# A piece of wq in a transfer of its own, and another order of the last steps, in a decode step of windowed attention with a gated MLP

## The chip, the cores and the metric

The kernel runs on one core of one Trainium2 chip. It is one launch: all inputs are in the chip's memory, the output of 4 KB goes back there. The metric is device time in microseconds (us), taken as the median of several runs. The profile is one execution recorded by the hardware profiler: which instruction ran when on TensorE (PE, with its weight loads PEld), VectorE (DVE), ScalarE (ACT), GpSimd (POOL) and SyncE (SP), what each waited for, and every packet that the 16 DMA engines moved.

## The reference

Two tokens (batch B = 2, one position each) of D = 512 pass through a layernorm, then two branches, all in float32:

```python
xn = _layernorm(x)                                   # 2 x 512
# A: attention of 32 query heads over 8 kv heads, last W = 4096 of 32768 positions
q = (xn @ wq)                                        # 512 x 4096, heads of 128
k = k_cache[:, :, Sk - W:, :]; v = v_cache[:, :, Sk - W:, :]
o = softmax(q @ k^T * 128 ** -0.5) @ v               # 4 query heads per kv head
s = o.reshape(B, 1, 4096) @ wo                       # 4096 x 512
# B: a gated MLP of 512 -> 1792 -> 896 -> 512
z = gelu(xn @ w_in); z1, z2 = halves(z); z2 = layernorm(z2) * w_sp + b_sp
g = silu((z1 * z2) @ w_out)
out = x + s * g
```

What must be read: 2 x 8 windows of K and of V at 2 MB each (64 MB), wq and wo at 8 MB each, w_in 3.5 MB, w_out 1.75 MB: some 89 MB. The arithmetic is small beside that.

## The kernel before

**Tiles and buffers.** The big loads go through a ring of four buffers of 32 KB a partition (`slot`): `win` (w_in), `wq0` and `wq2` (two of wq's four row sets each), the tiles `k` and `v` of eight units, `wo0` and `wo1`. `w_out` has a buffer of another pool. A unit is two of the sixteen (batch, kv head) pairs; its K and its V are 4 MB each, one transfer each (`load`, L134).

**wq.** Row 4p + k of wq lies on partition p (`wq_v`, L125), so each of the four sets k is 128 rows of 4096 columns. The layernormed x is transposed by four small PE transposes into `xnT` (L195 to L198), whose set k holds the same 128 rows; `queries(k)` (L262) multiplies set k with eight blocks of 512 columns and adds up over k in PSUM. wq0 (k = 0, 1) comes in one transfer of 4 MB, wq2 (k = 2, 3) in two of 2 MB:

```python
for k, n in ((0, 2),) if a == 0 else ((0, 1), (1, 1)):
    sp.dma_start(t[:, k : k + n], wq_v[:, a + k : a + k + n, :])
```

From PSUM the queries go through `qs`, `qx`, `xm` and a matmul `qa` into `qb` (`place_queries`, L327), the arrangement in which the score matmuls use them.

**A unit's steps.** `T` (`turn`, L373) transposes an eighth of K on DVE into `kts`; `shares` (L383) multiplies with `qb` on PE into `sh`; `keep` copies to `ss` on ACT; `scores` adds up on PE; `row_max`, `spread_max`, `share_max` and `bias` give the maximum; `exp` (`probs`) is ACT's, `probs_t` DVE's transpose into `pT`; `pv` (L451) multiplies with V into `acc` on PE; `own_sum`, `share_sum`, `weights` give 1/sum; `evacuate` scales on ACT, and `collect` and `gather` put the heads into `o1`.

**wo.** The 32 heads are split into three sets by kv head (`SETS`, L360): set 0 has kv heads 0 to 3 of both tokens, 16 rows of wo on each partition; sets 1 and 2 have two kv heads and 8 rows each. `spread` and `place` turn a set's `o1` into `oT`. `load_wo` (L511) gives out the transfers: set 0 in two halves of 2 MB (tile `wo0`), then in tile `wo1` set 1 in two halves of 1 MB and set 2 in blocks of 4, 2, 1 and 1 rows. `wo_early` (L523) multiplies sets 0 (steps `X`) and 1 (steps `Y`) with full rows of 512 columns into `part`, two rows a step; behind ORDER, the tail (L575 to L594) copies `part` to `parts`, multiplies set 2 into `so` and adds `parts` to it by a matmul with `rowm` after the first block. Then two DVE operations (gate, x) and the store.

**What sets the order.** The string `ORDER` (L27 to L52) lists all steps from unit 0 on; each engine runs its instructions in exactly that order (`InOrder`). `K:u`, `V:u` and `wo:n` stand in it too, and the SP engine gives out all big loads in this order: win, wout, wq, k0, k1, v0, k2, v1 and so on, v7, wo0, wo1. A load waits on SP until its ring buffer has been read for the last time: k2 takes the buffer of wq2 and waits for `queries(3)`, v7 waits for the last `T` of unit 6, wo0 for the last `pv` of unit 5, wo1 for the last `T` of unit 7. What stands behind a waiting load on SP waits too.

Of the kernel before, what the change touches and what calls it, by code (L numbers as in the profile page):

```python
# [9 lines left out]
F32 = mybir.dt.float32  # L10
AF = mybir.ActivationFunctionType
# [3 lines left out]
P = 128  # L15
HQ, DH = 32, 128
G = 4
# [3 lines left out]
def free_ap(t, offset, dims):  # L21

    return bass.AP(tensor=t.tensor, offset=t.offset + offset, ap=[list(t.ap[0])] + [list(d) for d in dims])
# [18 lines left out]
K:6 V:5 T:5.0 T:5.1 T:5.2 rowmax:4.1 mg:4 shmax:4 T:5.3 bias:4 shares:5.0 T:5.4 gather:3 exp:4.0 probs_t:4.0 T:5.5  # L42
T:5.6 exp:4.1 keep:5.0 pv:4.0 lsum:4 shsum:4 scores:5.0 T:5.7 shares:5.1 probs_t:4.1 pv:4.1 weights:4 keep:5.1
scores:5.1 evac:4 col:4 rowmax:5.0
K:7 V:6 T:6.0 rowmax:5.1 T:6.1 mg:5 T:6.2 shmax:5 T:6.3 T:6.4 bias:5 exp:5.0 exp:5.1 T:6.5 shares:6.0 probs_t:5.0
pv:5.0 lsum:5 T:6.6 keep:6.0 probs_t:5.1 T:6.7 shsum:5 scores:6.0 weights:5 shares:6.1 rowmax:6.0 pv:5.1
V:7 T:7.0 wo:0 keep:6.1 evac:5 scores:6.1 col:5 T:7.1 T:7.2 rowmax:6.1 mg:6 shmax:6 gather:5 spread:0 T:7.3 bias:6
T:7.4 T:7.5 shares:7.0 exp:6.0 probs_t:6.0 T:7.6 keep:7.0 pv:6.0 T:7.7 wo:1 exp:6.1 scores:7.0 shares:7.1 probs_t:6.1
keep:7.1 lsum:6 shsum:6 scores:7.1 rowmax:7.0 weights:6 pv:6.1 evac:6 rowmax:7.1 mg:7 shmax:7 col:6 oT:0 bias:7
gather:6 spread:1 exp:7.1 exp:7.0 probs_t:7.1 lsum:7 X:0.1 probs_t:7.0 X:0.3 X:0.2 shsum:7 weights:7 X:0.0 pv:7.0  # L50
pv:7.1 oT:1 evac:7 X:0.7 Y:0.1 X:0.4 X:0.5 col:7 Y:0.0 X:0.6 gather:7 spread:2 oT:2 Y:0.3 Y:0.2
"""  # L52


# [16 lines left out]
def kernel(  # L71
# [14 lines left out]
    pe, dve, act, sp = (InOrder(tc, e) for e in (nc.tensor, nc.vector, nc.scalar, nc.sync))  # L86
    B, _, D = x.shape
# [7 lines left out]
    KT = D // P  # L95
# [3 lines left out]
    DC = D // G  # L99
    SCALE = DH ** -0.5  # L100
    OFF = 30000.0 / SCALE

    fit = ctx.enter_context(tc.tile_pool(name="fit", bufs=1))
    fit.tile([P, 480], F32, tag="fit", name="fit")
# [2 lines left out]
    cst = ctx.enter_context(tc.tile_pool(name="cst", bufs=1))  # L107
    sb = ctx.enter_context(tc.tile_pool(name="sb", bufs=2))
    ps = ctx.enter_context(tc.tile_pool(name="ps", bufs=1, space=bass.MemoryType.PSUM))

    def slot(name, *shape):
        return ring.tile([P, *shape], F32, tag="slot", name=name)

    def bank(name, *shape):
        return ps.tile([P, *shape], F32, tag="kt", name=name, bufs=2)
# [9 lines left out]
    wq_v = wq.rearrange("(p k) f -> p k f", p=P)  # L125
    wqt = []
    for a in range(0, KT, 2):
        t = slot(f"wq{a}", 2, HQ * DH)
        for k, n in ((0, 2),) if a == 0 else ((0, 1), (1, 1)):
            sp.dma_start(t[:, k : k + n], wq_v[:, a + k : a + k + n, :])  # L130
        wqt += [t[:, 0], t[:, 1]]

    wb1 = cst.tile([1, 2], F32, tag="wb1", name="wb1")
# [12 lines left out]
    def load(u, src, name):  # L146
        t = slot(f"{name}{u}", UJ, DH)
        b, v = divmod(u, HKV // 2)
        first = src[b, 2 * v, SK - W, :]
        of = bass.AP(tensor=src.tensor, offset=first.offset, ap=[[UJ * DH, P // 2], [SK * DH, 2], [1, UJ * DH]])  # L150
        sp.dma_start(t.rearrange("p j d -> p (j d)"), of)
        return t


    ident = cst.tile([P, P], F32, tag="ident", name="ident")
    make_identity(nc, ident)
    selw = cst.tile([P, 60], F32, tag="selw", name="selw")
    nc.gpsimd.memset(selw, 0.0)
    xnT = cst.tile([P, KT, 32], F32, tag="xnT", name="xnT")
    nc.gpsimd.memset(xnT, 0.0)  # L160
    ones = cst.tile([P, P], F32, tag="ones", name="ones")
    nc.gpsimd.memset(ones, 1.0)
# [7 lines left out]
    rowm = cst.tile([P, 32], F32, tag="rowm", name="rowm")  # L170
# [21 lines left out]
    rsqrt(rs, va, "x")  # L192
    xn = sb.tile([B, D], F32, tag="o", name="xn", bufs=1)
    dve.tensor_scalar(xn, xs, mv[:, 0:1], rs, op0=ALU.subtract, op1=ALU.mult)
    pt = bank("xnT_ps", KT, B)  # L195
    for k in range(KT):
        pe.transpose(pt[:, k, :], xn.rearrange("b (p k) -> b k p", k=KT)[:, k, :], ident[:B, :B])
    dve.tensor_copy(xnT[:, :, :B], pt)  # L198

    same = cst.tile([P, G, 32], F32, tag="same", name="same")  # L200
# [15 lines left out]
    dve.tensor_reduce(other, free_ap(rowm, 0, [[4, 2], [8, REP]]), axis=AX.X, op=ALU.add)  # L216
    dve.tensor_scalar(other, other, -OFF, OFF, op0=ALU.mult, op1=ALU.add)
    diag = cst.tile([P, 4], F32, tag="diag", name="diag")
# [18 lines left out]
    for n in range(G):  # L237
        pz = bank(f"z{n}", 512)[:, :FC]
        for k in range(KT):
            pe.matmul(  # L240
                pz[32 * k : 32 * k + 32, :], xnT[:, k, :], win[:, k, n * FC : (n + 1) * FC],
                start=True, stop=True,
# [9 lines left out]
    pt = bank("zT_ps", 2, FT, B)  # L252
# [7 lines left out]
    pq = [ps.tile([P, 512], F32, tag=f"s{r}", name=f"q_ps{r}") for r in range(NR)]  # L260

    def queries(k):  # L262
        for r in range(NR):
            for g in range(G):
                c = (r * G + g) * 512
                pe.matmul(
                    pq[r][32 * g : 32 * g + 32, :], xnT[:, k, :], wqt[k][:, c : c + 512],
                    start=(k == 0), stop=(k == KT - 1),
                )

# [3 lines left out]
    u = cst.tile([P, 2, FT, B], F32, tag="u", name="u")  # L274
# [37 lines left out]
    for j in range(FT):  # L312
        for g in range(G):
            pe.matmul(
                y[32 * g : 32 * g + 32, :], hT[:, j, :], wout[:, j, g * DC : (g + 1) * DC],
                start=(j == 0), stop=(j == FT - 1),
# [20 lines left out]
    def place_queries():  # L337
        dve.tensor_tensor(
            free_ap(qb, 16, [[REP, G], [32, NP * G], [1, REP]]), free_ap(qa, 0, [[0, G], [REP, NP * G], [1, REP]]),
            free_ap(grpm, 0, [[1, G], [0, NP * G], [0, REP]]), op=ALU.mult,  # L340
        )

    gate = cst.tile([P, DC], F32, tag="gate", name="gate")

    def silu():
        dve.tensor_scalar(gate, ys, -1.0, 80.0, op0=ALU.mult, op1=ALU.min)
        act.activation(gate, gate, AF.Exp)
        dve.tensor_scalar_add(gate, gate, 1.0)
        dve.reciprocal(gate, gate)
        dve.tensor_mul(gate, gate, ys)  # L350
# [11 lines left out]
    for i, (kv, n, nj) in enumerate(SETS):  # L362
        o1 = cst.tile([P, B, 32], F32, tag=f"o1_{i}", name=f"o1_{i}")
        oT = cst.tile([P, nj, 32], F32, tag=f"oT_{i}", name=f"oT_{i}")
# [102 lines left out]
    col = {}  # L467
# [41 lines left out]
    blocks = []  # L509

    def load_wo(n):  # L511
        t = slot(f"wo{n}", 16, D)
        a = 0
        for i in ((0,), (1, 2))[n]:
            for j, n in (((0, 8), (8, 8)), ((0, 4), (4, 4)), ((0, 4), (4, 2), (6, 1), (7, 1)))[i]:
                sp.dma_start(t[:, a : a + n, :], wo_s[i][:, j : j + n, :])
                blocks.append((t[:, a : a + n, :], sets[f"oT{i}"][1], j))
                a += n
# [4 lines left out]
    def wo_early(n, at):  # L523
        nonlocal done
        if done == 0:
            part.append(ps.tile([P, 512], F32, tag="s0", name="part"))
        t, oT, j = blocks[n]
        for a in range(at, at + 2):
            g = done % G
            pe.matmul(  # L530
                part[0][32 * g : 32 * g + 32, :], oT[:, j + a, :], t[:, a, :], start=(done < G), stop=(done >= EARLY - G)
            )
            done += 1

    part = []
    STEPS = dict(
        T=turn, rowmax=row_max, mg=spread_max, shmax=share_max, bias=bias, exp=probs, probs_t=probs_t, lsum=own_sum,
        shsum=share_sum, weights=weights, shares=shares, keep=keep, scores=scores, pv=pv, evac=evacuate, col=collect,
        gather=gather,
    )  # L540

    def step(name, u, a=()):
        if name == "q":
            place_queries()
        elif name == "silu":
            silu()
        elif name == "K":
            units[u].k = load(u, k_cache, "k")
        elif name == "V":
            units[u].v = load(u, v_cache, "v")  # L550
        elif name == "wo":
            load_wo(u)
        elif name == "spread":
            spread(u)
        elif name == "oT":
            place(u)
        elif name == "X":
            wo_early(a[0] // 4, 2 * (a[0] % 4))
        elif name == "Y":
            wo_early(2 + a[0] // 2, 2 * (a[0] % 2))  # L560
        else:
            STEPS[name](units[u], *a)

    units = []
    for u in range(NU):
        p = Unit()
        p.u, p.m, p.kt, p.sh, p.ss, p.s, p.p, p.pT = u, None, {}, {}, {}, {}, {}, {}
        units.append(p)
    for line in ORDER.strip().split("\n"):
        for name in line.split():  # L570
            name, at = name.split(":")
            u, _, a = at.partition(".")
            step(name, int(u), (int(a),) if a else ())

    parts = sb.tile([P, D], F32, tag="o", name="parts", bufs=1)  # L575
    act.activation(parts, part[0], AF.Copy)
    so = bank("so", DC)
    for n in range(4, len(blocks)):
        t, oT, j = blocks[n]
        for a in range(t.shape[1]):  # L580
            for g in range(G):
                pe.matmul(
                    so[32 * g : 32 * g + 32, :], oT[:, j + a, :], t[:, a, g * DC : (g + 1) * DC],
                    start=(j + a == 0), stop=(j + a == oT.shape[1] - 1),
                )
        if n == 4:
            for g in range(G):
                pe.matmul(
                    so[32 * g : 32 * g + 32, :], rowm, parts[:, g * DC : (g + 1) * DC], start=False, stop=False
                )  # L590
    res = cst.tile([P, DC], F32, tag="res", name="res")
    dve.tensor_mul(res, so, gate)
    dve.tensor_add(res, res, x4)
    sp.dma_start(bass.AP(tensor=out.tensor, offset=out.offset, ap=by_group), res[0 : P : P // (G * B), :])  # L594

# [27 lines left out]
```

## Time and profile before

| | us |
|---|---|
| median of 3 runs (lowest, highest) | 217.93 (217.32, 218.16) |
| the profiled execution's own time | 217.48 |
| its span, first to last instruction | 215.7 |
| PE busy | 143.5 (67%) |
| DVE busy | 126.3 (59%) |
| ACT busy | 50.9 (24%) |
| queue q1 (loads), share of 16 DMA engines' span | 96.6% |
| moved | 89.56 MB, mean 415 GB/s |
| PE's last matmul ends | 212.2 |

The page cuts the span into 40 equal slices and gives a digit of the busy share for each engine, the clock that PE was granted and the mean share of the 16 DMA engines; the windows do the same for any stretch. The chain of waits goes back from the last instruction through what released each. In the timeline, instructions of a group are on one line with start and length; where SP is listed (SPq), the line tells when transfers were given out, not when they moved. A packet is the piece of a transfer that one DMA engine moves as a unit: here one partition's bytes.

### The profile page before, as it was taken

To read this page: it belongs to the slowest core of one execution; us is meant where nothing else is said; L and a number is where in the kernel's file an instruction comes from. 1 tells how busy PE (TensorE), PEld (TensorE's weight loads), DVE (VectorE), ACT (ScalarE), POOL (GpSimd) and SP (SyncE) were. 2 spreads that over 40 slices of the span, in tenths; PEclk is the share of its full clock that TensorE was granted. 3 is DMA by queue.
4 is the path that set the end of the run, shared out by engine and by line. 5 is a ranking of instruction groups with operands and counts; after the bars stand their busy time and mean duration, and the time that the engine had idled before them with its cause. 6 is when DMAs were issued, how large, how long until landed. Compare 5 with 4: busy or idle time off the path is not lost.

```text
span 215.7 us, 2477 instructions
## 1 busy us (share of the span) xinstructions
PE 143.5 (67%) x972; PEld 51.6 (24%) x972; DVE 126.3 (59%) x217; ACT 50.9 (24%) x128; POOL 5.2 (2%) x19
## 2 busy tenths in 40 slices
PE   0179694722864895954990796389168939975993
PEld 0128521300111232312220221122112322221342
DVE  2511212259598989849918972993698199534001
ACT  4111203200114236023330603142032305242020
POOL 8000000000000000000000000000000000000000
PEclk9998578785589699995796589579955985997999
DMA  6999999999999999999999999999999999999990
GB/s 256 426 438 444 407 428 468 395 463 407 462 413 441 431 425 444 419 448 407 456 413 456 419 441 431 419 444 422 450 409 462 407 450 419 441 401 428 419 376 23
DMA packets 4219, 89.56 MB, mean 415 GB/s; under 512 B 478, under 2 KB 494, under 8 KB 880
## 3 DMA queue, kind: packets, MB, share of 16 engines
q1 hardware_dynamic: 4188, 89.40, 96.6%
q8 instruction: 8, 0.13, 0.2%
q10 hardware_dynamic: 20, 0.01, 0.0%
q14 instruction: 3, 0.02, 0.0%
HBM read 89.40 MB, written 0.00 MB: 414 GB/s over the span
## 4 chain that ended last, share of the span: by engine, by line
DMA 57%; PE 20%; DVE 17%; ACT 4%; issue 1%; ACTq 0%
DMA k<-in_A_k_cache_dram 40%; DMA wo<-in_A_wo_dram 12%; DVE kts L65 11%; PE acc L65 7%; DMA win<-in_B_w_in_dram 5%; PE sh L65 5%; PE part L65 4%; ACT p L65 3%; PE s L65 3%; DVE pT L65 2%; DVE m L65 1%; PE so L65 1%; DVE gate L65 1%; DVE nb L65 1%; ACT ss L65 1%
## 5 line engine op out<-in xcount | busy, mean ns | idle before, releaser
L65 DVE STREAM_TRANSPOSE kts<-k 128x1024 f32<-128x1024 f32 x64 | 75.7, 1219 | 25.7 <-DMA k<-in_A_k_cache_dram 25.7
L65 PE MATMUL sh<-kts,qb 128*32 128x512 f32 x256 | 42.9, 793 | 12.5 <-DVE kts L65 9.0
L65 PE MATMUL acc<-v,pT 128*32 128x512 f32 x256 | 36.4, 676 | 6.9 <-DVE pT L65 4.0
L65 ACT ACTIVATE p<-s,nb 128x512 f32<-128x512 f32 x32 | 22.5, 730 | 38.6 <-DVE nb L65 38.6
L65 ACT ACTIVATE ss<-sh 128x512 f32<-128x512 f32 x16 | 9.6, 599 | 61.4 <-PE sh L65 61.4
L65 DVE STREAM_TRANSPOSE pT<-p 128x1024 f32<-128x1024 f32 x16 | 19.6, 1226 | 2.5 <-ACT p L65 2.5
L65 PE MATMUL s<-ss,sums 128*128 128x512 f32 x32 | 18.8, 671 | 2.1 <-ACT ss L65 2.1
L65 PE MATMUL mo<-mg,joint 128*128 128x16 f32 x16 | 4.2, 338 | 23.6 <-DVE mg L65 23.6
L65 PEld LDWEIGHTS acc<-v,pT 128*32 128x32 f32 x256 | 11.4, 143 | 32.6 <-issue 21.8
L65 PEld LDWEIGHTS sh<-kts,qb 128*32 128x32 f32 x256 | 8.8, 128 | 35.1 <-issue 31.1
L65 DVE TENSOR_REDUCE m<-s 128x1 f32<-128x512 f32 x16 | 10.8, 678 | 5.9 <-PE s L65 5.8
L65 PE MATMUL q_ps<-wq,xnT 128*32 128x512 f32 x64 | 11.0, 820 | 4.6 <-DMA wq<-in_A_wq_dram 4.6
L65 ACT ACTIVATE o<-acc,wd 128x128 f32<-128x128 f32 x32 | 9.1, 367 | 19.5 <-PE acc L65 19.5
L65 PE MATMUL part<-wo,oT 128*32 128x512 f32 x48 | 9.5, 709 | 2.4 <-DMA wo<-in_A_wo_dram 2.4
L65 PEld LDWEIGHTS mo<-mg,joint 128*128 128x128 f32 x16 | 3.3, 261 | 26.8 <-DVE mg L65 24.2
L65 PE MATMUL z<-win,xnT 128*32 128x448 f32 x32 | 5.2, 814 | 3.9 <-DMA win<-in_B_w_in_dram 3.9
L65 PEld LDWEIGHTS s<-ss,sums 128*128 128x128 f32 x32 | 5.0, 197 | 10.4 <-issue 7.4
L65 PE MATMUL zT_ps<-rowm,z 128*128 128x2 f32 x28 | 6.6, 370 | 0.0
L65 PEld LDWEIGHTS zT_ps<-rowm,z 128*128 128x128 f32 x28 | 6.5, 325 | 0.0
L65 ACT ACTIVATION_READ_ACCUMULATOR p<-s,nb 128x1 f32 x32 | 6.4, 200 | 0.0
L65 ACT ACT_TABLE_LOAD x4 | 5.1, 1283 | 2.6 <-POOL hT L164 2.6
L65 PE MATMUL xnT_ps<-ident,xn 2*128 2x2 f32 x4 | 0.6, 253 | 7.5 <-DVE xn L65 7.5
(108 smaller groups left out, 71.4 us busy)
## 6 DMA issues: line engine op xcount, KB each, us to landing
k<-in_A_k_cache_dram SPq DMA_DIRECT2D x8, 4096.0 KB, 23.8
v<-in_A_v_cache_dram SPq DMA_DIRECT2D x8, 4096.0 KB, 29.8
wq<-in_A_wq_dram SPq DMA_DIRECT2D x1, 4096.0 KB, 24.3
wq<-in_A_wq_dram SPq DMA_DIRECT2D x2, 2048.0 KB, 29.4
wo<-in_A_wo_dram SPq DMA_DIRECT2D x2, 2048.0 KB
win<-in_B_w_in_dram SPq DMA_DIRECT2D x1, 3584.0 KB
wo<-in_A_wo_dram SPq DMA_DIRECT2D x3, 1024.0 KB, 24.3
wout<-in_B_w_out_dram SPq DMA_DIRECT2D x1, 1792.0 KB, 15.0
```

Of the source, the lines that this page charges most:

```text
L65: return self.tc.keep_in_program_order(call(*args, **kwargs))
```

## The change

Three things are edited.

First, wq2 is loaded in another cut: one transfer of 30 KB a partition (all but the last 512 columns of set k = 3), and one of 2 KB a partition for those columns. The source of the second is written with 8 as its outermost dimension: 8 times 16 rows, with steps 4 and 32 rows of wq, so that partition 16c + d gets row set position c + 8d. The same rows in another order need x in the same order: `xn8` is a DVE copy of that column set of `xn` in the permuted order, a fifth PE transpose puts it into a fifth set of `xnT`, and `queries(3)` uses it for the last of its eight blocks.

Second, `load_wo` gives out set 0 in one transfer of 4 MB and set 1 in one of 2 MB, six transfers in place of eight.

Third, the last lines of ORDER, from unit 7's K on, are in another order, and the tail has become steps of ORDER: `parts` (copy), `Z` (one block of set 2), `pz` (adding `parts`). `pv:7.0` and `pv:7.1` stand ahead of all `X`; `spread:0` and `spread:1` stand together; `pz` stands after the second block of set 2, no longer after the first.

```diff
-K:7 V:6 T:6.0 rowmax:5.1 T:6.1 mg:5 T:6.2 shmax:5 T:6.3 T:6.4 bias:5 exp:5.0 exp:5.1 T:6.5 shares:6.0 probs_t:5.0
-pv:5.0 lsum:5 T:6.6 keep:6.0 probs_t:5.1 T:6.7 shsum:5 scores:6.0 weights:5 shares:6.1 rowmax:6.0 pv:5.1
-V:7 T:7.0 wo:0 keep:6.1 evac:5 scores:6.1 col:5 T:7.1 T:7.2 rowmax:6.1 mg:6 shmax:6 gather:5 spread:0 T:7.3 bias:6
-T:7.4 T:7.5 shares:7.0 exp:6.0 probs_t:6.0 T:7.6 keep:7.0 pv:6.0 T:7.7 wo:1 exp:6.1 scores:7.0 shares:7.1 probs_t:6.1
-keep:7.1 lsum:6 shsum:6 scores:7.1 rowmax:7.0 weights:6 pv:6.1 evac:6 rowmax:7.1 mg:7 shmax:7 col:6 oT:0 bias:7
-gather:6 spread:1 exp:7.1 exp:7.0 probs_t:7.1 lsum:7 X:0.1 probs_t:7.0 X:0.3 X:0.2 shsum:7 weights:7 X:0.0 pv:7.0
-pv:7.1 oT:1 evac:7 X:0.7 Y:0.1 X:0.4 X:0.5 col:7 Y:0.0 X:0.6 gather:7 spread:2 oT:2 Y:0.3 Y:0.2
+K:7 V:6 T:6.0 rowmax:5.1 mg:5 T:6.1 T:6.2 shmax:5 bias:5 T:6.3 exp:5.0 T:6.4 exp:5.1 T:6.5 probs_t:5.0 shares:6.0
+keep:6.0 lsum:5 shsum:5 scores:6.0 probs_t:5.1 T:6.6 T:6.7 rowmax:6.0 pv:5.0 weights:5 shares:6.1 keep:6.1 pv:5.1
+V:7 T:7.0 wo:0 scores:6.1 rowmax:6.1 T:7.1 T:7.2 mg:6 T:7.3 shmax:6 bias:6 T:7.4 evac:5 col:5 exp:6.0 exp:6.1 T:7.5
+probs_t:6.0 T:7.6 T:7.7 wo:1 lsum:6 shares:7.0 keep:7.0 pv:6.0 scores:7.0 shares:7.1 rowmax:7.0 keep:7.1 shsum:6
+scores:7.1 probs_t:6.1 weights:6 rowmax:7.1 mg:7 pv:6.1 evac:6 shmax:7 gather:5 col:6 bias:7 exp:7.0 gather:6 exp:7.1
+probs_t:7.0 spread:0 probs_t:7.1 lsum:7 spread:1 pv:7.0 shsum:7 oT:0 weights:7 pv:7.1 X:0.6 X:0.0 oT:1 X:0.2 X:0.4
+evac:7 X:0.3 col:7 X:0.7 gather:7 spread:2 X:0.5 Y:0.1 Y:0.0 Y:0.3 X:0.1 Y:0.2 parts:0 oT:2 Z:0 Z:1 pz:0 Z:2 Z:3
...
+    LAST = 512
...
-        for k, n in ((0, 2),) if a == 0 else ((0, 1), (1, 1)):
-            sp.dma_start(t[:, k : k + n], wq_v[:, a + k : a + k + n, :])
+        if a == 0:
+            sp.dma_start(t, wq_v[:, a : a + 2, :])
+        else:
+
+            of, to = wq_v[:, a : a + 2, :].rearrange("p k f -> p (k f)"), t.rearrange("p k f -> p (k f)")
+            n = 2 * HQ * DH - LAST
+            sp.dma_start(to[:, :n], of[:, :n])
+            at = wq.offset + KT * HQ * DH - LAST
+            by_8 = [[KT * HQ * DH, 8], [8 * KT * HQ * DH, 16], [1, LAST]]
+            sp.dma_start(to[:, n:], bass.AP(tensor=wq.tensor, offset=at, ap=by_8))
...
+    xn8 = cst.tile([B, 8, 16], F32, tag="xn8", name="xn8")
+    dve.tensor_copy(xn8, xn.rearrange("b (d c k) -> b c d k", c=8, k=KT)[:, :, :, KT - 1])
...
+    pe.transpose(pt[:, KT, :], xn8.rearrange("b c d -> b (c d)"), ident[:B, :B])
...
+                rows = KT if k == KT - 1 and c >= HQ * DH - LAST else k
...
-                    pq[r][32 * g : 32 * g + 32, :], xnT[:, k, :], wqt[k][:, c : c + 512],
+                    pq[r][32 * g : 32 * g + 32, :], xnT[:, rows, :], wqt[k][:, c : c + 512],
...
-            for j, n in (((0, 8), (8, 8)), ((0, 4), (4, 4)), ((0, 4), (4, 2), (6, 1), (7, 1)))[i]:
+            for j, n in (((0, 16),), ((0, 8),), ((0, 4), (4, 2), (6, 1), (7, 1)))[i]:
...
+    def copy_parts():
+        parts.append(sb.tile([P, D], F32, tag="o", name="parts", bufs=1))
+        act.activation(parts[0], part[0], AF.Copy)
+
+    def wo_last(n):
+        if n == 0:
+            so.append(bank("so", DC))
+        t, oT, j = blocks[2 + n]
+        for a in range(t.shape[1]):
+            for g in range(G):
+                pe.matmul(
+                    so[0][32 * g : 32 * g + 32, :], oT[:, j + a, :], t[:, a, g * DC : (g + 1) * DC],
+                    start=(j + a == 0), stop=(j + a == oT.shape[1] - 1),
+                )
+
+    def add_parts():
+        for g in range(G):
+            pe.matmul(
+                so[0][32 * g : 32 * g + 32, :], rowm, parts[0][:, g * DC : (g + 1) * DC], start=False, stop=False
+            )
```

More of the change, by code (lines that the diff above doesn't have):

```diff
@@ L158 @@
     nc.gpsimd.memset(selw, 0.0)
-    xnT = cst.tile([P, KT, 32], F32, tag="xnT", name="xnT")
+    xnT = cst.tile([P, KT + 1, 32], F32, tag="xnT", name="xnT")
     nc.gpsimd.memset(xnT, 0.0)
@@ L194 @@
     dve.tensor_scalar(xn, xs, mv[:, 0:1], rs, op0=ALU.subtract, op1=ALU.mult)
-    pt = bank("xnT_ps", KT, B)
+    xn8 = cst.tile([B, 8, 16], F32, tag="xn8", name="xn8")
+    dve.tensor_copy(xn8, xn.rearrange("b (d c k) -> b c d k", c=8, k=KT)[:, :, :, KT - 1])
+    pt = bank("xnT_ps", KT + 1, B)
     for k in range(KT):
         pe.transpose(pt[:, k, :], xn.rearrange("b (p k) -> b k p", k=KT)[:, k, :], ident[:B, :B])
+    pe.transpose(pt[:, KT, :], xn8.rearrange("b c d -> b (c d)"), ident[:B, :B])
     dve.tensor_copy(xnT[:, :, :B], pt)
@@ L535 @@
     part = []
+    def copy_parts():
[16 more added lines that the diff above has]
+            )
+    parts, so = [], []
     STEPS = dict(
@@ L557, in step @@
         elif name == "X":
-            wo_early(a[0] // 4, 2 * (a[0] % 4))
+            wo_early(0, 2 * a[0])
         elif name == "Y":
-            wo_early(2 + a[0] // 2, 2 * (a[0] % 2))
+            wo_early(1, 2 * a[0])
+        elif name == "Z":
+            wo_last(u)
+        elif name == "parts":
+            copy_parts()
+        elif name == "pz":
+            add_parts()
         else:
@@ L573 @@
             step(name, int(u), (int(a),) if a else ())
[L575 to L590, printed above, removed]
     res = cst.tile([P, DC], F32, tag="res", name="res")
-    dve.tensor_mul(res, so, gate)
+    dve.tensor_mul(res, so[0], gate)
     dve.tensor_add(res, res, x4)
```

## The prediction

> **What bounds the kernel now.** I read the page's strip of slices and table of queues first, then the windows and chain at the end, then the packets of the trace engine by engine.
>
> ```profile
> DMA  6999999999999999999999999999999999999990
> q1 hardware_dynamic: 4188, 89.40, 96.6%
> q8 instruction: 8, 0.13, 0.2%
> q14 instruction: 3, 0.02, 0.0%
> ```
>
> From the second slice to the last but one the 16 DMA engines are full; q1, the loads, fills 96.6% of their span. In the packets, each engine starts the next one 3 to 4 ns before the last ends, from 2.0 us on. Start to start, a 32 KB packet takes 1209 ns, a 16 KB one 607, 2 KB 80, a semaphore 5.6; between 28 KB (1059) and 32 KB, 30 KB comes to 1134. The compute has no part in the length of this queue, so only bytes, packet counts and their spread over engines can move its end.
>
> The spread is uneven, as the end of the queue shows:
>
> ```profile
> 209.00:209.50 0.50, 0.18 (x1) 1.00 0.88 348
> 209.50:210.00 0.50, 0.00 (x0) 1.00 0.60 234
> 210.00:210.50 0.50, 0.00 (x0) 1.00 0.54 209
> 210.50:211.00 0.50, 0.00 (x0) 1.00 0.27 102
> 211.00:211.50 0.50, 0.00 (x0) 1.00 0.05 20
> ```
>
> The last two columns are the DMA share and GB/s in stretches of half a microsecond. Between 210.0 and 210.5 half of the engines are done. Followed packet by packet, eight engines end at 209.11 to 210.01 and eight at 210.63 to 211.24. What makes them late are instruction fetches. q8 carries 16 KB at 30.0, 68.6, 92.8, 128.0, 149.7, 186.5 and 204.5 (and at 212.0, when the loads are over), each on another engine; such a packet takes 0.88 to 0.97 us and the engine's next load packet is 0.46 to 0.55 longer, 1.42 in all. q14 carries 8 KB at 46.8, 95.4 and 159.0, the first and third on one engine: 1.69 together. Seven engines with a q8 fetch and the one with two q14 fetches are the late eight.
>
> ```profile
> 171.43 25.47 DMA wo<-in_A_wo_dram
> 196.89 0.14 issue
> 197.03 3.56 PE part L65 x12
> ...
> 210.10 2.12 PE so L65 x72
> ```
>
> This chain of waits says that after wo's first half lands (196.89) PE runs without a gap to the end. The last landing is 211.54; with the 0.14 of issue and the last 8 `so` (0.27) a chain bound by transfers ends at 211.95. PE ends at 212.18, so its queue costs 0.23. From there 5.3 us (two 0.29 DVE operations, the store, the end) lead to the profiled 217.48, which is 0.45 under the median of 217.93. Sums are made against 217.48 and then moved by 0.45.
>
> **The eight-engine transfer.** It takes the last 256 KB of wq2 out of a 16-engine transfer: 128 rows of 2 KB, with 8 outermost in the source. No earlier transfer has 8 there, but the small ones of x show the rule: outer dimension 1 uses one engine, 2 two, 4 four, and the smaller sets lie inside the larger. So I take 8 engines with 16 packets each. Before, an engine spent 2 x (8 x 607.06 + 5.6) = 9724 ns on wq2. After, a taken engine spends 8 x 1134.1 + 5.6 + 16 x 80.04 + 5.6 = 10365 ns, +0.64; the other eight 9078, -0.65, and they go on with K0's packets at once. Merging wo's first transfers saves, twice, 16 KB packet pairs for 32 KB ones or 8 KB for 16 KB: 8 x (2 x 607.06 - 1209.4) + 5.6 = 43 ns on set 0 and about as much on set 1. At the end: +0.55 on taken engines, -0.73 on the others.
>
> Which eight? The four of x's transfers end at 209.53, 209.72, 210.01 and 210.90; the last is the one with two q14 fetches, the other three are on time. The other four are not in the trace. Of the twelve left, five are on time and seven late. Since none of the four had a q8 fetch before the loads' end, and all eight q8 fetches fell on different engines, I take it that the q8 fetches keep to the other eight. Then the last packets are 210.90 + 0.55 = 211.45 on the taken engines and 211.24 - 0.73 = 210.51 on the rest. Last landing 211.54 + 0.21 = 211.75. The bounds: were the latest engine taken too, 211.24 + 0.55 = 211.79; were no late engine taken, 210.01 + 0.55 = 210.56.
>
> The trace has a row that speaks for an even load: all engines full to 209. [...]
>
> **wq2 arriving as one piece.** queries(2) started at 32.11 on the first half; now it waits for 30 KB, about 35.9 (one 16 KB half more, 4.9 us, less what 2 KB spare). Both queries then run from 35.9: at the rates of the rows before (16 in 1.92 at full, 3.48 at half clock) they end at 41.3 with the half-clock window where it was, 42.9 if all at half, against 40.24. qa is then done 1.1 to 2.6 later than 45.17. qb at 47.58 stands on DVE behind K0's first transpose (46.41 to 47.66), which waits for K0's landing: 46.3 against 47.8 costs nothing to 0.2, in a chain that reaches the loads only through slots: k2 waits for queries(3) with over 20 us to spare. xn8 (a DVE copy of 2x128) and a fifth transpose: nearest rows 0.17 to 0.3 and 0.15; PE waits for win 3.94 after them, so nothing. Without that cover, under half a microsecond.
>
> **SP's queue.** Its order of loads stays:
>
> ```profile
> 150.19 16.50 SPq L65 DMA_DIRECT2D v<-in_A_v_cache_dram  x2
> 171.43 20.97 SPq L65 DMA_DIRECT2D wo<-in_A_wo_dram  x8
> ```
>
> v7 is given out at about 166.7, wo0 at 171.43, wo1 by 192.4; the engines reach them 10 us or more later. T:6.7, which frees v7's slot, passes two or three DVE steps of 0.1 to 1.2, under 4 us. Two DMAs fewer on SP gain nothing. POOL gains only a longer clear of xnT, beside win's wait.
>
> **The order of the end.** wo0 now lands whole, so X starts at its end instead of 197.03: the second half landed at 201.7 before, and the latest taken engine, then 0.3 to 0.4 ahead of the last, is now 0.60 later, so about 201.9. In return acc7 (32 of 3.9 us) goes ahead of X, in the time in which PE waited. At full clock, what is left after 202.03 is 32 X and 16 Y at 0.107, col 0.42, oT_ps 1.0, 64 `so` at 0.033 and `rowm` 0.30: 8.97, to 211.0 if nothing had to be waited for. Set 1 lands at about 206.8, the first block of set 2 at 209.2, the next at 210.5, the last at 211.75, so PE waits at each and the transfers set the end: 211.75 + 0.14 + 0.27 = 212.16, against 212.18. PE's slack is 1.15.
>
> ```profile
> 193.56:196.97 3.41, 1.06 (x8) 1.00 0.98 418
> 196.97:200.39 3.42, 3.36 (x12) 0.50 1.00 426
> 200.39:203.80 3.41, 3.41 (x32) 1.00 0.98 416
> ```
>
> These windows (PE's busy time, granted clock) show the danger: after a window with 1.06 of work the next is granted 0.50, and does 12 matmuls where a full one does 32. A whole half-clock window on X costs 20 x 0.107 = 2.1, less the slack +1.0. The gap ahead of X is 3.1 us at worst (acc7 ending 199, if both probabilities are turned by 196.76). The windows at 190.15 (2.06 of work) and 39.96 (1.8) kept the clock. With acc7 and `mo` in it, 196.97 to 200.39 has 1.9 to 3, so I take full clock. [...]
>
> **Sum.** 212.16 - 212.18 = -0.02 on 217.48, or 217.9 as a median: no change.
>
> **Rivals.**
> R1, the eight engines stay clear of fetches: another sequence of instructions on the q14 engine, whose fetches then fall elsewhere or once. The last packet falls to about 210.6, landing 210.9, end 211.3: -0.85, 217.05. For it: the fetch's engine is not tied to the load. Against: three fetches went to two engines, the same one first and third.
> R2, the other four are among the late: 211.79 and, with a fetch more on one of them in the new program, to 212.1. End +0.3 to +0.6: 218.2 to 218.5. For it: seven of twelve unknown engines are late. Against: the four known ones never carried q8.
> R3, slower: the gap ahead of X, at another phase of the clock's windows, fills most of one, and X runs at half clock. From 1.8 us of half clock on it decides: +0.4, a whole window +1.0 (218.9), a second one over +2 (above 220). For it: the rows above. Against: the work counted there.
> R4, the transfer takes 16 engines anyway: only -0.09 and PE's 0.23 are left, 217.6. Against: x's transfers.
>
> **Chances.** Forecast 0.45; R1 0.17; R2 0.17; R3 0.14; R4 0.04; anything else 0.03. Half a per cent (1.1 us) is about what a measurement of this kernel can tell from no change: faster means under 216.84, slower over 219.02. R1 with the median's own scatter (217.32 to 218.16) gives faster 0.13 in all; R3's upper half, some of R2 and the rest give slower 0.17; same 0.70. The range goes from R1 less 0.3 to R3's whole window: 216.75 to 219.0; the forecast's own is 217.4 to 218.3.
>
> **What would show it.** Right: a 256 KB transfer as 16 packets of 2 KB on each of eight engines, near 36 us; the two groups' ends within 1 us of each other; last landing 211.6 to 211.9; PE idle ahead of X and again ahead of `so`. R1: landing under 211. R2: a late engine among the eight. R3: granted 0.50 with X in it. Wrong altogether: K0's or v7's packets with gaps ahead of them on q1.

## The result, and the profile after

The changed kernel is slower: 218.80 us (median of 9 runs, 218.34 to 220.14) against 217.61 (9 runs, 217.25 to 218.42). The ratio is 1.0058, with a 95% interval of 1.004 to 1.0077: about 1.2 us lost. The forecast was no change, 217.9; the time lies inside the stated range, near its upper end, but outside the forecast's own 217.4 to 218.3. The profiled execution took 218.80 with a span of 216.8, against 217.48 and 215.7: 1.32 us more. Of the runs of the kernel before that the experiments below use, two took 316 us and are left out of every comparison.

The page of the changed kernel has the same full strip, with one fetch on q8 less:

```profile
DMA  7999999999999999999999999999999999999980
q1 hardware_dynamic: 3892, 89.40, 96.7%
q8 instruction: 7, 0.11, 0.2%
q14 instruction: 3, 0.02, 0.0%
```

The bytes are the same, and they took longer. The windows at the end, in the same stretches as before (the last two columns are DMA share and GB/s):

```profile
209.50:210.00 0.50, 0.00 (x0) 1.00 0.85 340
210.00:210.50 0.50, 0.00 (x0) 1.00 0.84 328
210.50:211.00 0.50, 0.00 (x0) 1.00 0.75 295
211.00:211.50 0.50, 0.00 (x0) 1.00 0.36 139
211.50:212.00 0.50, 0.00 (x0) 1.00 0.19 74
212.00:212.50 0.50, 0.00 (x0) 1.00 0.15 57
212.50:213.00 0.50, 0.00 (x0) 1.00 0.02 8
```

The engines are done later than before (a share of 0.84 between 210.0 and 210.5, where it was 0.54), by 0.9 us in the mean of their last packets, and a few go on to 212.66, where the last packet ended at 211.24. That is 1.42 us later, and PE's last matmul ends 1.32 later, at 213.54 instead of 212.22.

The loss is already there early on. DVE's first transpose of K0 waits for K0's landing; its line in the timeline is this one before the change,

```profile
46.41 1.25 DVE L65 STREAM_TRANSPOSE kts<-k 128x1024 f32<-128x1024 f32 x1 [2.52 <-DMA k<-in_A_k_cache_dram]
```

and this one after it:

```profile
47.60 1.25 DVE L65 STREAM_TRANSPOSE kts<-k 128x1024 f32<-128x1024 f32 x1 [3.57 <-DMA k<-in_A_k_cache_dram]
```

K0 is complete 1.19 us later, at 22% of the span, long before the new order of the end begins. In the packets between 33.8 and 36.6 us the reason can be seen. Of the 128 packets of 2 KB, 16 on each of eight engines as forecast, 38 take at most 86 ns (mostly 84, which is the 80 from start to start that I had priced), most others 130 to 160, the longest 213; together 16.1 us instead of 10.8. And the other engines' first K0 packets of 32 KB, which take 1.21 us in every kernel without such a transfer, take 1.9 to 2.2 us, and their second ones 1.3 to 1.7. The eight that carry the small packets have slow K0 packets behind them too (1.4 to 1.8). Over all 16 engines the large packets are 12.1 us too long; this sum is called their excess below, and leaves out some 0.5 us that an instruction fetch at 36.1 adds to one of them. With the 5.3 us of the small ones that is 17.4 us, or 1.09 an engine, which no term of the sum had.

At the end PE had no time to spare either, and this chain shows why:

```profile
197.54 1.26 DVE pT L65
198.79 0.04 issue
198.84 3.51 PE acc L65 x16
202.35 0.31 PE mo L65 x2
202.66 1.88 PE acc L65 x16
204.54 1.84 PE part L65 x17
```

The last unit's `acc` started at 198.84; in the kernel called sixteen below, which differs only in the transfer of 256 KB, it starts at 197.11. Its first half ran at half clock (3.51 us for 16, then 1.88 for 16; 3.50 in sixteen, too). X began right behind it at 204.4. PE did not wait for wo0, as I had it do from 199 to 202.

### The profile page after: what moved, and what is told of

It is laid out like the page before. It is cut to its first block, busy times and chain, and to the rows that moved or that the text cites. A ratio compares the mean times of both kernels' runs of the same rounds, so it can differ in the third digit from the quotient of the medians.

```text
span 216.8 us, 2479 instructions
## 1 busy us (share of the span) xinstructions
PE 145.3 (67%) x973; PEld 51.2 (24%) x973; DVE 126.2 (58%) x218; ACT 51.1 (24%) x128; POOL 5.2 (2%) x19
## 4 chain that ended last, share of the span: by engine, by line
DMA 62%; PE 26%; DVE 6%; ACT 3%; issue 1%; ACTq 0%
DMA v<-in_A_v_cache_dram 41%; DMA k<-in_A_k_cache_dram 17%; PE acc L65 11%; PE sh L65 7%; DMA win<-in_B_w_in_dram 5%; PE s L65 4%; DVE kts L65 3%; PE part L65 2%; DVE pT L65 1%; ACT p L65 1%; PE so L65 1%; ACT ss L65 1%; DVE gate L65 1%; PE mo L65 1%; ACT o L65 1%
## 5 line engine op out<-in xcount | busy, mean ns | idle before, releaser
L65 PE MATMUL acc<-v,pT 128*32 128x512 f32 x256 | 37.8, 712 | 7.8 <-DVE pT L65 4.9
L65 PE MATMUL s<-ss,sums 128*128 128x512 f32 x32 | 19.5, 691 | 2.4 <-ACT ss L65 2.4
L65 PEld LDWEIGHTS acc<-v,pT 128*32 128x32 f32 x256 | 10.4, 144 | 32.7 <-issue 22.7
L65 DVE TENSOR_REDUCE m<-s 128x1 f32<-128x512 f32 x16 | 10.8, 675 | 9.2 <-PE s L65 9.1
L65 PE MATMUL q_ps<-wq,xnT 128*32 128x512 f32 x64 | 11.4, 859 | 3.4 <-DMA wq<-in_A_wq_dram 3.4
L65 PE MATMUL z<-win,xnT 128*32 128x448 f32 x32 | 6.1, 938 | 4.0 <-DMA win<-in_B_w_in_dram 4.0
L65 PEld LDWEIGHTS s<-ss,sums 128*128 128x128 f32 x32 | 5.4, 213 | 11.9 <-issue 9.0
L65 PE MATMUL part<-wo,oT 128*32 128x512 f32 x48 | 5.8, 594 | 0.0
L65 DVE COPY z<-z 128x448 f32<-128x448 f32 x2 | 1.2, 625 | 7.4 <-PE z L65 7.4
```

The lines of the kernel that those rows point to most:

```text
L65: return self.tc.keep_in_program_order(call(*args, **kwargs))
```

## The experiments

Two questions were open: which part of the change costs, and what in the eight-engine transfer is slow. The first four kernels (wq only, order and whole sets, sixteen, together) ran on one chip with 31 runs of the kernel before (median 217.99), the next four (order alone, whole sets alone, small first, quarters) on another with 27 (217.93), and own and others once each on a third. These times include what an execution spends outside its span, 1.7 to 3.5 us here; where that matters, the median of the spans is given too.

**Each part alone.**

```diff
 # wq only: before.py with the two transfers of wq2, xn8, the fifth transpose; ORDER and wo as before
-        for k, n in ((0, 2),) if a == 0 else ((0, 1), (1, 1)):
-            sp.dma_start(t[:, k : k + n], wq_v[:, a + k : a + k + n, :])
...
+            sp.dma_start(to[:, :n], of[:, :n])
...
+            sp.dma_start(to[:, n:], bass.AP(tensor=wq.tensor, offset=at, ap=by_8))
...
```

> Only wq2's two transfers, xn8 and the fifth transpose; wo's transfers and ORDER as before. Theory (the changed kernel's packets show it: the 2 KB packets took 81 to 213 ns, most of them 130 to 160, and not the 84 that I priced, and the eight other engines' first K0 packets 1.6 to 2.2 us and not 1.21): this transfer alone holds up all 16 engines by about 1 us, so this kernel ends about where the changed one does, 1.0 to 1.6 us over before (ratio 1.005 to 1.007). Rival (the new order or the whole sets of wo cost it): within 0.3 us of before.

Measured: 219.45, ratio 1.0067 (1.004 to 1.0095). It has the slow packets (mean 125 ns; 11.9 us of excess in the large ones) and K0's first transpose at 47.60. The transfer costs the whole loss.

```diff
 # order and whole sets: after.py with wq2 in two halves again, no xn8
...
-            sp.dma_start(to[:, :n], of[:, :n])
...
-            sp.dma_start(to[:, n:], bass.AP(tensor=wq.tensor, offset=at, ap=by_8))
+        for k, n in ((0, 2),) if a == 0 else ((0, 1), (1, 1)):
+            sp.dma_start(t[:, k : k + n], wq_v[:, a + k : a + k + n, :])
...
```

> Only the new order of the end and wo's whole sets; wq2 in two halves as before, no xn8. Theory (the 256 KB transfer costs all of it): within 0.4 us of before, rather below it, since wo has two transfers fewer (0.09 us an engine) and PE's 0.23 us behind the last landing may go. Rival: 1.0 us or more above before.

Measured: 217.04, ratio 0.9962 (0.9942 to 0.9982): faster than both kernels. So the change consists of a gain of 0.4% and a loss of 1.0%. In its chain of waits the end hangs on the last transfer and no longer on PE's queue:

```profile
185.61 25.71 DMA wo<-in_A_wo_dram
211.37 0.47 PE so L65 x8
211.86 0.30 DVE res L65
```

**Which half of that gain.**

```diff
 # order only: as the last one, but wo's sets 0 and 1 in halves
-            for j, n in (((0, 16),), ((0, 8),), ((0, 4), (4, 2), (6, 1), (7, 1)))[i]:
+            for j, n in (((0, 8), (8, 8)), ((0, 4), (4, 4)), ((0, 4), (4, 2), (6, 1), (7, 1)))[i]:
...
```

> Only the new order of the end; wo's sets in halves as before, wq2 in two halves. If the order is what gains the 0.4% that order and whole sets gain together (PE keeps more slack behind the last landing, whatever its clock): 0.3 to 1.0 us under before. If the whole sets gain it: within 0.3 us of before.

```diff
 # whole sets only: before.py, its ORDER, with wo's sets 0 and 1 whole
-            for j, n in (((0, 8), (8, 8)), ((0, 4), (4, 4)), ((0, 4), (4, 2), (6, 1), (7, 1)))[i]:
+            for j, n in (((0, 16),), ((0, 8),), ((0, 4), (4, 2), (6, 1), (7, 1)))[i]:
...
```

> Only wo's sets whole (six transfers), in the order of before, in which four X stand ahead of the last unit's pv on PE. X now waits for the whole set, about 201.7 instead of 196.9, and acc7 (3.9 us of PE work at full clock) behind it: PE has all its 48 part, 32 acc and 64 so left at 202, 13 us of work. Expected by this sum: PE ends near 215, 2.5 to 4 us slower than before. If the order is worth nothing: within 0.4 us of before.

Measured: order alone 217.35, ratio 0.9972 (0.9957 to 0.9987), so the order makes most of it; what the whole sets add to it (0.1%) is within the intervals. Whole sets without the new order: 222.73, ratio 1.0212 (1.0183 to 1.0242), 4.8 us slower. My sum had 2.5 to 4. In its timeline PE stands idle 7.4 us before X, and then its whole queue is still ahead:

```profile
201.69 3.36 PE L65 MATMUL part<-wo,oT 128*32 128x512 f32 x12 [7.40 <-DMA wo<-in_A_wo_dram]
```

The first 12 of X are at half clock (3.36 us; the granted clock was 0.50 from 194.41 to 204.65). The sum had all of them at full clock, a difference of 2 us: the half-clock window that I had feared for X, in the old order. The two edits belong together: whole sets alone cost 4.8 us, and nothing with the order that puts `acc` ahead of X.

**Eight engines, or pieces of 2 KB.**

```diff
 # sixteen: after.py, the small transfer with 128 rows outermost, usual row order
-            at = wq.offset + KT * HQ * DH - LAST
-            by_8 = [[KT * HQ * DH, 8], [8 * KT * HQ * DH, 16], [1, LAST]]
-            sp.dma_start(to[:, n:], bass.AP(tensor=wq.tensor, offset=at, ap=by_8))
+            sp.dma_start(to[:, n:], of[:, n:])
...
-                rows = KT if k == KT - 1 and c >= HQ * DH - LAST else k
+                rows = k
```

> The changed kernel, but the 256 KB go in a transfer with all 128 rows outermost, in their usual order (xn8 and its transpose are still made and not used). 16 engines with 8 packets of 2 KB each. If eight engines alone is what hurts: 2 KB packets of 84 ns again, K0's first packets 1.21 us, and the time falls to within 0.4 us of before. If it is the pieces themselves (2 KB at a stride of 64 KB) that are slow beside other loads: 2 KB packets of 130 ns or more here too, and 0.5 us or more of the loss stays.

Measured: 217.16, ratio 0.9963 (0.9939 to 0.9987). All 128 small packets take 84 ns, K0's 1213. The pieces are harmless when 16 engines carry them. The time is 0.8 us under the kernel before, and not within 0.4 of it, since the order and the whole sets gain here too. K0's first transpose is back at

```profile
46.40 1.25 DVE L65 STREAM_TRANSPOSE kts<-k 128x1024 f32<-128x1024 f32 x1 [1.27 <-DMA k<-in_A_k_cache_dram]
```

**Where the pieces are read.**

```diff
 # together: after.py, the source one piece of 256 KB
-            at = wq.offset + KT * HQ * DH - LAST
-            by_8 = [[KT * HQ * DH, 8], [8 * KT * HQ * DH, 16], [1, LAST]]
+            at = wq.offset
+            by_8 = [[LAST, 8], [8 * LAST, 16], [1, LAST]]
```

> The changed kernel, but the eight-engine transfer reads the first 256 KB of wq in one piece of memory (steps of 2 and 16 KB instead of 64 and 512 KB), into the same partitions; so the last block of queries is made from other numbers than the reference's. If the sources' stride of 64 KB makes the packets slow: 84 ns a packet, K0's packets 1.21 us, and 0.7 us or more of the loss is gone. If it is where they are written, or that two transfers are under way on different engines: packets of 130 to 160 ns and the time of the changed kernel within 0.3 us.

Measured: 219.17, ratio 1.0054 (1.0032 to 1.0076); mean 123 ns, 11.2 us of excess, as in the changed kernel. The time is 0.37 over the changed kernel's, at nearly the same span (medians 216.7 and 216.6). The stride of the source has no part in it.

**What runs beside it.**

```diff
 # small first: after.py, the two transfers of wq2 swapped
-            sp.dma_start(to[:, :n], of[:, :n])
...
             sp.dma_start(to[:, n:], bass.AP(tensor=wq.tensor, offset=at, ap=by_8))
+            sp.dma_start(to[:, :n], of[:, :n])
```

> The changed kernel, with the eight-engine transfer given out ahead of the 30 KB one, so that it runs beside wq's 30 KB packets and not K0's. Theory (partitions written): the same conflict with another neighbour, 2 KB packets of 130 ns or more, 30 KB packets longer than 1138 ns by 0.3 us or more, time within 0.4 us of the changed kernel. Rival (K0's rows are what it conflicts with): 84 ns, and the time within 0.4 us of the version with 16 engines.

Measured: 218.58, ratio 1.0032 (1.0016 to 1.0048). Now wq's 30 KB packets are slow, 11.4 us of excess in all, and the small ones take 120 ns on average. So it is not K0's rows. By its ratio the time falls between the two bounds, nearer to the changed kernel; the median span is the changed kernel's (216.65 against 216.6).

**Where the pieces are written.** This leaves the destination. The trace doesn't record partitions; from the order of the source I take it that each of the eight engines of the changed kernel writes 16 neighbouring ones. If the destination decides, another spread of the same pieces over the partitions has to change the packets.

```diff
 # quarters: after.py, four transfers of 32 partitions; xn8's order to match
...
-            sp.dma_start(to[:, n:], bass.AP(tensor=wq.tensor, offset=at, ap=by_8))
+            row = KT * HQ * DH
+            for p0 in range(0, P, 32):
+                by_8 = [[row, 8], [8 * row, 4], [1, LAST]]
+                at = wq.offset + p0 * row + row - LAST
+                sp.dma_start(to[p0 : p0 + 32, n:], bass.AP(tensor=wq.tensor, offset=at, ap=by_8))
...
```

> The changed kernel, but the 2 KB pieces go in four eight-engine transfers of 32 partitions each (0 to 31, 32 to 63, 64 to 95, 96 to 127), so that each engine writes 4 neighbouring partitions of a quarter, and not 16; rows permuted inside a quarter, xn8 to match. Bytes, packets and engines are those of the changed kernel. [...] Rival (two transfers at once on different engines slow each other whatever they write): all packets at 130 to 160 ns but the first few, and the loss of the changed kernel stays, 1.5 us or more over the version with 16 engines.

Measured: 218.59, ratio 1.0027 (1.0011 to 1.0043). 107 of the 128 packets take 84 ns, only the last eighth 149 on average; the large packets' excess falls from 12.1 to 7.0 us, and all together from 1.09 to 0.51 us an engine. So the packets go with the destination, against the rival, though the loss over sixteen, some 1.4 us, is near the rival's 1.5. The median span, 216.5, is hardly below the changed kernel's 216.6, so the argument rests on the packets here and not on the time. By the order of the four transfers the slow eighth is the last to be written, into 64 to 127. So the halves were taken apart:

```diff
 # own: only partitions 0 to 63, 4 KB each in pieces of 2 KB     # others: the same with 64 to 127
-    LAST = 512
+    LAST = 1024
...
+            nc.gpsimd.memset(to[64 : 64 + 64, n:], 0.0)         # others: to[0 : 0 + 64, n:]
+            for m in range(n, n + LAST, 512):
+                for p0 in range(0, 0 + 64, 32):                 # others: range(64, 64 + 64, 32)
+                    by_8 = [[row, 8], [8 * row, 4], [1, 512]]
+                    at = wq.offset + p0 * row + row - LAST + m - n
+                    sp.dma_start(to[p0 : p0 + 32, m : m + 512], bass.AP(tensor=wq.tensor, offset=at, ap=by_8))
...
```

> The kernel with quarters, but with 4 KB a partition instead of 2, in pieces of 2 KB, and only for partitions 0 to 63 (four eight-engine transfers of 32 partitions, 128 packets, 16 an engine, 256 KB, as in the changed kernel). The last 1024 columns of set 3 are not loaded for partitions 64 to 127, but zeroed, so the queries' last two blocks lack half of their rows; 256 KB less are loaded in all. [...] Rival (any eight-engine transfer slows the others): packets of 130 ns and more, and 4 us or more of excess in the large packets together.

> [...] Theory: 2 KB packets of 130 ns and more once the other engines are in K0, and 8 us or more of excess in the large packets together. Rival: the same as in the one before.

One run of each: 217.72 us for own, 218.51 for others (64 to 127 loaded, 0 to 63 zeroed), 217.97 for the kernel before. Number of engines and of packets, bytes and neighbours are the same; the partitions differ, and with them the rows that are read. Into 0 to 63, all 128 packets take 84 ns, and the 32 KB packets beside them take 1213, against the rival. Into 64 to 127, the mean is 127 ns (the later five eighths 137 to 160) and the large packets have 12.0 us of excess. Here too the first 50 still take 84 ns: the slowing starts some 0.6 us after the first packet. In quarters, too, 43 of the 64 packets to the upper half are at 84 ns. The window from 33.8 to 36.6 us shows it in the last column, GB/s; first own, then others:

```profile
33.80:36.60 2.80, 1.30 (x7) 1.00 1.08 455
```

```profile
33.80:36.60 2.80, 1.30 (x7) 1.00 1.17 331
```

and the same window in the changed kernel and in sixteen:

```profile
33.80:36.60 2.80, 1.30 (x7) 0.68 1.26 357
```

```profile
33.80:36.60 2.80, 1.30 (x7) 0.98 1.11 467
```

The DMA share is over 1 in others and in the changed kernel as well: the engines are busy, and move less. K0's first transpose, in own and then in others, tells the same:

```profile
45.75 1.25 DVE L65 STREAM_TRANSPOSE kts<-k 128x1024 f32<-128x1024 f32 x1 [2.76 <-DMA k<-in_A_k_cache_dram]
```

```profile
47.26 1.25 DVE L65 STREAM_TRANSPOSE kts<-k 128x1024 f32<-128x1024 f32 x1 [5.17 <-DMA k<-in_A_k_cache_dram]
```

The packets of all kernels with such a transfer, put together (the large packets' excess is over 1213 or 1138 ns, all 16 engines, without the 0.5 us that an instruction fetch adds):

| kernel | 2 KB packets of at most 86 ns, of 128 | mean ns | excess of large packets, us | ratio to before |
|---|---|---|---|---|
| changed kernel | 38 | 126 | 12.1 | 1.0058 |
| wq only | 38 | 125 | 11.9 | 1.0067 |
| together | 46 | 123 | 11.2 | 1.0054 |
| small first | 54 | 120 | 11.4 | 1.0032 |
| quarters | 107 | 93 | 7.0 | 1.0027 |
| sixteen | 128 | 84 | 0.0 | 0.9963 |
| own | 128 | 84 | 0.0 | one run |
| others | 50 | 127 | 12.0 | one run |

So with eight engines it is the partitions written that decide in these kernels, and not the rows read: sixteen reads the changed kernel's rows without a loss. An instruction fetch (q8) falls into the slow stretch of five of these kernels, at 35.3 to 36.1 us, but isn't the cause: small first has none there (its slow stretch begins at 24.9, the fetch comes at 30.5) and the same excess, and order and whole sets has one at 34.7 and only one packet longer by 0.5 us.

The half alone doesn't explain all: in the changed kernel 90 of the 128 small packets take more than 86 ns and only 64 go to partitions 64 to 127, so at least 26 of these 90 go to 0 to 63, where own has none. Own writes 0 to 63 in transfers of 32 partitions, the changed kernel all 128 in one; which engine writes which partitions, and what it is that slows them there, no run shows.

## Why the prediction was wrong

*Which engines, how many packets.* Right: eight engines with 16 packets of 2 KB each, near 34 to 36 us, and the four of x's transfers among them.

*"A taken engine spends ... 16 x 80.04"* and *"the other eight ... go on with K0's packets at once"*. This is the step that failed. The 80 ns came from packets of 16-engine transfers; the row was taken over to a transfer in which eight engines write all 128 partitions. In its place the runs showed 126 ns on average and large packets beside and behind it that are up to 1.0 us too long: 1.09 us an engine, as a mean over all 16, given back by no one. Undoing that alone (sixteen) takes the ratio from 1.0058 to 0.9963, 2.1 us (1.2 to 3.0 by the intervals' bounds); between the medians of the spans it is 1.35 (216.6 and 215.25), and between the last packets of the two profiles 1.47. The sum on a taken engine would have been 1.73: 1.09 for the excess and the 0.64 for eight packets more.

*The last packet, 211.45 on the engine with two q14 fetches.* The engine was the right one; it ended at 212.66. Its small packets were 0.59 us too long and its first K0 packet 0.53. Without these 1.12 it would have ended at 211.54. So the balance of extra work against fetches was computed rightly and is worth nothing here, as forecast.

*"The q8 fetches keep to the other eight."* Wrong. In the changed kernel two of seven q8 fetches, at 94.4 and 116.6, fell on taken engines, which ended at 212.13 and 212.59. R2 had this; by itself it would have brought the end to about 211.5, too. In quarters and in small first there were two such fetches as well, at other times. Which engine a fetch falls on differed from kernel to kernel.

*"+0.64; the other eight 9078, -0.65".* The other eight do go on, but slowly, and the loss was above the +0.64 (sixteen is 1.35 shorter by the spans). The number of engines alone doesn't make it: own had eight engines and no slow packet, so the reason is the place of the writes.

*wq2 in one piece.* Right in its cost: K0's first transpose has qb behind it as before, and in sixteen it stands at 46.40 (46.41 before), though queries waited for the whole piece.

*The order of the end, -0.02 with the transfer, "-0.09 and PE's 0.23" without.* Mis-sized to the other side: without the transfer the rest gains 0.4% (0.2 to 0.6%), 0.4 to 1.3 us, and not 0.3. The order makes most of it. The kernel before has runs from 216.98 to 219.36, the one with order and whole sets from 216.72 to 217.64. Their spans tell the same, 215.2 to 217.0 (median 216.2) and 214.9 to 215.3 (median 215.15), so gain and scatter both lie inside the span. That PE's queue ended late by more than 0.23 in many executions of the kernel before, by the phase of the clock's windows (the granted clock changes at steps of 3.41 us in the trace), would explain both, but is only argued: one execution is profiled, and no run here fixed the phase.

*R3, X at half clock.* Not so; `acc` had the half-clock window and X followed it without a gap. The gap ahead of X that I had drawn at 199 to 202 was filled by `acc` at half clock. So the step "I take full clock" failed too: it rested on windows with 1.8 and 2.06 us of work that had kept the clock, and here the window from 195.25 to 198.66 had 1.90 and the next was granted 0.50. This is not what cost the time: sixteen has the same (1.91, then 0.50) and still ends on its last transfer.

## What to carry to other kernels

As far as these runs go, a transfer on eight engines has to be judged by the partitions that it writes. Into 64 to 127 both sides were slowed (2 KB packets of 127 ns on average, 12.0 us of excess in the large ones), and the 84 ns taken from 16-engine transfers didn't hold; into 0 to 63 it did, with no excess. So before work is moved from late DMA engines to early ones, a run has to show the packet times into the partitions that it is moved to. When a change has parts, run each alone: here a gain of 0.4% was hidden under a loss of 1.0%, and the version with order and whole sets, wq2 in halves as before, is the one to keep (217.04, ratio 0.9962).

## What the runs showed that I had not expected

With the engines full (a DMA share of 1.17 and 1.08 between 33.8 and 36.6 us), 331 GB/s were moved where the small packets went into the upper half of the partitions (others), and 455 where they went into the lower (own): a full strip of DMA is no proof of full rate. And with whole sets in the old order, PE's wait of 7.4 us was followed by 12 matmuls in 3.36 us at a granted clock of 0.50, where the window from 200.39 to 203.80 of the kernel before had 32 in 3.41 us at 1.00, and an edit of transfers alone cost 4.8 us.
